# First batch of a long convolution: loads further ahead, products made earlier and shared by two engines, half of a sign change on another engine

## The chip, the cores and the metric

One Trainium2 chip, one of its cores. TensorE (PE) multiplies matrices into PSUM; VectorE (DVE), ScalarE (ACT) and GpSimd (POOL) work element by element; SyncE (SP) and GpSimd issue the DMAs here. Each engine takes its instructions in the order in which the program lists them, and waits on semaphores of the others. The metric is the device time of one execution in microseconds; less is better.

## The reference

A long convolution over the sequence, multiplied by x, and a feed-forward net with a squared ReLU behind it:

```python
h_filt = (np.maximum(pos_emb @ w1, 0.0) @ w2) * np.exp(-0.01 * pos)[:, None]
u = x * v                                    # batch 4, seq 12480, d_model 128
Uf = np.fft.rfft(u, n=2 * S, axis=1)
Hf = np.fft.rfft(h_filt, n=2 * S, axis=0)
y = np.fft.irfft(Uf * Hf[None], n=2 * S, axis=1)[:, :S]
x = (x * y).reshape(B * S, D)
out = np.maximum(x @ w_in, 0.0) ** 2 @ w_out # 128 -> 2048 -> 128
```

All of it is in fp32.

## The kernel before

The sequence is padded to 112 x 112, and the transform is made of matmuls with tables of 112 x 112, in stages over one large SBUF tile `W`. Each fp32 operand is split into a high and a low part, and a product is three matmuls (`mm3`, lines 75 to 77). The order at the start of the program is: the filter's small net (`filter_mlp`), the filter's stage one (`stage1(None, True, ...)`, called `s1f`), the filter's stage two (`stage2(True, True, ...)`, `s2f`), the first batch's stage one (`stage1(0, True, ...)`, `s1`), its stage two, stage three, and then the feed-forward net, between whose steps the other batches' stages run. Only the filter's and the first batch's stages have nothing else beside them ("big").

Stage one goes over 32 blocks of 4 channels, 112 x 4 x 112 floats each. For a block of the first batch: `load` fetches xt and vt (lines 236, 237, SP's queue), `mul` makes u = x v in place of xt (244), `prep` makes the high part on ACT (254), `prep2` the low part on VectorE (262), `mm` issues 12 matmuls into two PSUM banks, and `evac` copies both banks into `W`, the first on ACT (282), the second on VectorE (280) where the stage is "big". The filter's stage one has no loads and no products. Stage two goes over 56 blocks. In the filter's, a block is: a half-precision table (load 344) widened on VectorE (`widen`, 363), a block of `W` split into high part (`prep`, ACT, 385) and low part (`prep2`, VectorE, 393), its real part's sign changed (`neg`: line 401 on GpSimd for the filter, 403 on ACT otherwise), 12 matmuls, and a copy by ACT (423) that is stored to `Hd` (424). `prep` and `prep2` run two blocks ahead of the matmuls.

No planner sets the order: the stages are Python generators, and whoever advances one with `step` places its next section in every engine's queue at that point. A `hook` is called at the end of each block with t - n, so t == -28 is block 4 of 32 in stage one and t == -3 is block 53 of 56 in stage two. Before the first block, stage one has sections that end in a `yield`: the first loads; then the first products and the remaining early loads; then the first `prep`; then the first `prep2`. In the kernel before, the filter's stage one places the first section of `s1`, and block 53 of the filter's stage two the second one, with three products.

Of the kernel before, what the change touches and what calls it, by code (L numbers as in the profile page):

```python
# [7 lines left out]
F32 = mybir.dt.float32  # L8
# [9 lines left out]
I = 112  # L18
# [14 lines left out]
def hyena_moe_kernel(  # L33
# [19 lines left out]
    nc = tc.nc  # L53
# [12 lines left out]
    def pool(name, side="left", **kw):  # L66
        return tc.tile_pool(name=name, bufs=kw.pop("bufs", 2), side=side, reuse_waits="tile", **kw)

    def bank():
        return psf.tile([128, 512], F32, tag="F", name="F")  # L70

    def mm3(o, L, R, first=True, last=True):
        lh, ll = L
        rh, rl = R
        nc.tensor.matmul(o, lh, rh, start=first, stop=False)  # L75
        nc.tensor.matmul(o, lh, rl, start=False, stop=False)  # L76
        nc.tensor.matmul(o, ll, rh, start=False, stop=last)  # L77

    def load_tab(p, src, k):
        t = p.tile([I, k, 2 * I], F32R, name="tab", bufs=1)  # L80
        nc.gpsimd.dma_start(out=t, in_=src)
        return t
# [50 lines left out]
    def by_value():  # L133
        return W.rearrange("p t (c d) -> p (t c) d", c=4)
# [4 lines left out]
    def first_rows():  # L139
        return W.rearrange("p t (q d) -> p (t q) d", q=4)[:, :I].rearrange("p (e s) (c k) -> p c e s k", e=4, k=4)  # L140
# [73 lines left out]
    def rest(k):  # L214
        for _ in range(k):
            yield 1
            yield 2
            yield 3

    def stage1(b, big, et=None, side="left", hook=None):  # L220
        DC = 4
        n = D // DC
        with pool("s1", side) as p:
            if et is None:
                et = load_tab(p, e_tab, 2)
            E = (et[:, 0, :], et[:, 1, :])
            ext = 3 if big else 0
            pa = (3 if b is None else 2) if big else 1
            L = {}

            def load(t):
                if b is None or t >= n:
                    return
                xt = p.tile([I, DC, I], F32, tag="xt", name="xt", bufs=2 + pa + ext)
                vt = p.tile([I, DC, I], F32, tag="vt", name="vt", bufs=2 + ext)
                nc.sync.dma_start(out=xt, in_=xs[b, :, t * DC : (t + 1) * DC, :])
                nc.sync.dma_start(out=vt, in_=vs[b, :, t * DC : (t + 1) * DC, :])
                L[t] = xt, vt

            def mul(t):  # L240
                if b is None or t >= n:
                    return
                xt, vt = L[t]
                nc.gpsimd.tensor_mul(out=xt, in0=xt, in1=vt)

            def like(x):
                return x if b is not None else x.rearrange("p d (s k) -> p d s k", k=4)

            def prep(t):
                if t >= n:  # L250
                    return
                u = first_rows()[:, t] if b is None else L.pop(t)[0]
                hi = p.tile([I, DC, I], F32R, tag="uh", name="uh", bufs=1 + pa)
                nc.scalar.copy(like(hi), u)
                q[t] = u, hi

            def prep2(t):
                if t >= n:
                    return
                u, hi = q[t]  # L260
                lo = p.tile([I, DC, I], F32R, tag="ul", name="ul", bufs=1 + pa)
                nc.vector.tensor_sub(out=like(lo), in0=u, in1=like(hi).bitcast(F32))
                q[t] = hi, lo

            def mm(t):
                hi, lo = q.pop(t)
                A = []
                for h in range(DC // 2):
                    A.append(bank())
                    for k in range(2):  # L270
                        mm3(A[h][:I, k * 2 * I : (k + 1) * 2 * I], (hi[:, 2 * h + k, :], lo[:, 2 * h + k, :]), E)
                return A

            def evac(t, A):
                for h in range(DC // 2):
                    d0 = t * DC + 2 * h
                    dst = by_value()[:, :, d0 : d0 + 2]
                    src = A[h][:I, : 4 * I].rearrange("p (d t) -> p t d", d=2)
                    if big and h:
                        nc.vector.tensor_copy(dst, src)  # L280
                    else:
                        nc.scalar.copy(dst, src)

            q = {}
            la = 2 + pa + ext
            early = min(la, 2 + ext)
            for t in range(early):
                load(t)
            if big:
                yield 1  # L290
            else:
                yield from rest(1)
            for t in range(pa + 1):
                mul(t)
            for t in range(early, la):
                load(t)
            yield 1
            for t in range(pa):
                prep(t)
            yield 2  # L300
            for t in range(pa):
                prep2(t)
            prev = None
            for t in range(n):
                yield 1
                load(t + la)
                mul(t + pa + 1)
                if prev is not None:
                    evac(t - 1, prev)
                prep(t + pa)  # L310
                yield 2
                prep2(t + pa)
                yield 3
                prev = mm(t)
                if hook is not None:
                    hook(t - n)
            yield 1
            evac(n - 1, prev)

    def stage2(filt, big, side="left", ring=None, hook=None):  # L320
        n = I // 2
        TK = 2 if big and not filt else 1
        pa = 2 if big else 1
        lag = 2 if big else 1
        la = (4 if filt else 2 * (NTB - 1)) if big else 2
# [3 lines left out]
        def whole(t):  # L329
            return big and not filt and (t // TK % 2 == 1 or t >= n - 4)  # L330
# [24 lines left out]
        with pool("s2", side) as p:  # L355
# [39 lines left out]
            def neg(t):  # L395
                if t >= n or whole(t):
                    return
                a = q[t].rearrange("p h k r d -> p (h k) r d")
                src = a[:, :, 0, :].bitcast(F32)
                if filt:  # L400
                    nc.gpsimd.tensor_scalar(out=a[:, :, 2, :], in0=src, scalar1=-1.0, scalar2=1.0, op0=ALU.mult, op1=ALU.mult)
                else:
                    nc.scalar.mul(a[:, :, 2, :], src, -1.0)
# [49 lines left out]
            for t in range(pa):  # L453
                neg(t)
            prev = {}
            for t in range(n + lag):
                yield 1
                load(t + la)
                load_h(t + lh)
                prep(t + pa)  # L460
                yield 2
                if not big:
                    prep2(t + pa)
                if t - lag in prev:
                    post(t - lag, prev.pop(t - lag))
                if big:
                    prep2(t + pa)
                    widen(t + pa)
                yield 3
                neg(t + pa)  # L470
                if t < n:
                    prev[t] = mm(t)
                if hook is not None:
                    hook(t - n)
# [59 lines left out]
    def stage4(b, done, ring=None):  # L534
        L, X, q, Y, Z = {}, {}, {}, {}, {}

# [93 lines left out]
    def fft(b, done):  # L630
        yield from stage1(b, False)
        yield from stage2(False, False)
        yield from stage3(False)
        yield from stage4(b, done)
# [19 lines left out]
    def step(gen, k=1):  # L654
        for _ in range(k):
            next(gen, None)
# [4 lines left out]

    filter_mlp(tables)
    et = tabs[0]
    s1f = stage1(None, True, et, "right", lambda t: t == -28 and step(s1))
    s2f = stage2(True, True, "right", half, lambda t: t == -3 and step(s1))
    s1 = stage1(0, True, et, "left", lambda t: t == -3 and step(s2))
    step(s2f)
    run(s1f)
# [238 lines left out]
```

## Time and profile before

| | us |
|---|---|
| median of 3 runs | 3440.4 (3438.72 to 3444.68) |
| profiled execution | 3440.29 |
| its span, first to last instruction | 3438.5 |

Over the span TensorE is busy 99%, VectorE 82%, ScalarE 79%, GpSimd 40%; the mean granted clock is 0.993. The first 340 us hold the filter and the first batch; what follows is mostly the feed-forward net. Times in rows are microseconds, the start of an instruction counted from the span's start; an instruction's time holds what it waits for inside the engine, and in square brackets stands the idle time before it with what ended it.

### The profile page before, as it was taken

To read this page: it belongs to the slowest core of one execution; us is meant where nothing else is said; L and a number is where in the kernel's file an instruction comes from. 1 tells how busy PE (TensorE), PEld (TensorE's weight loads), DVE (VectorE), ACT (ScalarE), POOL (GpSimd) and SP (SyncE) were. 2 spreads that over 40 slices of the span, in tenths; PEclk is the share of its full clock that TensorE was granted. 3 is DMA by queue.
4 is the path that set the end of the run, shared out by engine and by line. 5 is a ranking of instruction groups with operands and counts; after the bars stand their busy time and mean duration, and the time that the engine had idled before them with its cause. 6 is when DMAs were issued, how large, how long until landed. Compare 5 with 4: busy or idle time off the path is not lost.

```text
span 3438.5 us, 58656 instructions
## 1 busy us (share of the span) xinstructions
PE 3390.6 (99%) x20986; PEld 3197.9 (93%) x20986; DVE 2830.0 (82%) x3328; ACT 2717.6 (79%) x4014; POOL 1370.2 (40%) x1448
## 2 busy tenths in 40 slices
PE   8998999999999999999999999999999999999999
PEld 8987999999999989999999999999999999999998
DVE  7989877889887777879887777788887777788888
ACT  6765778887778878887777788888777788888887
POOL 2578055349920045339940035436960015400000
PEclk9999999999999999999999999999999999999999
DMA  2899155446610055436630035445640025400000
GB/s 77 260 252 248 51 142 146 124 124 178 181 54 17 17 137 146 121 116 179 183 86 17 17 100 145 126 125 151 183 137 17 17 60 146 125 27 25 25 25 20
DMA packets 211892, 371.90 MB, mean 108 GB/s; under 512 B 26448, under 2 KB 156816, under 8 KB 211600
## 3 DMA queue, kind: packets, MB, share of 16 engines
q1 hardware_dynamic: 158736, 242.89, 24.1%
q0 software_dynamic: 52864, 125.27, 14.0%
q8 instruction: 166, 2.72, 0.3%
q14 instruction: 126, 1.03, 0.1%
HBM read 242.64 MB, written 64.00 MB: 89 GB/s over the span
## 4 chain that ended last, share of the span: by engine, by line
PE 86%; issue 8%; DVE 3%; DMA 1%; POOL 1%; ACT 1%; SPq 0%; DVEq 0%; POOLq 0%; ACTq 0%
PE F L75 11%; PE F L76 11%; PE F L77 11%; PE A L75 10%; PE A L77 10%; PE A L76 9%; PE O L75 8%; PE O L76 8%; PE O L77 8%; PE F L594 1%; DVE m L433 1%; DMA ht<-Hd 1%; PE F L593 1%; DVE W L433 1%; DMA vt<-vs 0%
## 5 line engine op out<-in xcount | busy, mean ns | idle before, releaser
L722 ACT ACTIVATE r<-A 128x892 f32<-128x892 f32 x896 | 821.8, 917 | 304.9 <-PE A L77 93.1
L725 DVE SCALAR_TENSOR_TENSOR A<-A,r 128x892 f32<-128x892 f32 x723 | 791.4, 1095 | 297.5 <-ACT r L722 295.3
L724 ACT ACTIVATE gh<-r 128x892 fp32r<-128x892 f32 x896 | 852.0, 951 | 186.2 <-PE O L77 179.6
L735 DVE TENSOR_TENSOR gl<-A,gh 128x892 fp32r<-128x892 f32 x723 | 786.0, 1087 | 143.2 <-ACT gh L724 120.2
L75 PE MATMUL A<-zh,wt 128*128 128x446 f32 x1792 | 675.6, 377 | 3.7 <-DVE gl L735 1.8
L77 PE MATMUL A<-zh,wt 128*128 128x446 f32 x1792 | 653.6, 365 | 0.0
L76 PE MATMUL A<-zl,wt 128*128 128x446 f32 x1792 | 651.7, 364 | 0.0
L541 POOL DMA_DIRECT2D tb<-t x224 | 123.9, 554 | 1083.4 <-PE F L77 828.6
L75 PE MATMUL O<-gh,wt 128*128 128x446 f32 x1456 | 529.5, 364 | 0.0
L77 PE MATMUL O<-gh,wt 128*128 128x446 f32 x1456 | 529.5, 364 | 0.0
L76 PE MATMUL O<-gl,wt 128*128 128x446 f32 x1456 | 529.3, 364 | 0.0
L75 PEld LDWEIGHTS A<-zh,wt 128*128 128x128 f32 x1792 | 344.3, 192 | 25.6 <-DVE gl L735 8.2
L77 PEld LDWEIGHTS A<-zh,wt 128*128 128x128 f32 x1792 | 336.8, 188 | 23.3
L76 PEld LDWEIGHTS A<-zl,wt 128*128 128x128 f32 x1792 | 340.1, 190 | 15.0 <-DVE zl L707 0.4
L567 POOL TENSOR_TENSOR al<-W,ah 112x512 fp32r<-112x512 f32 x212 | 288.0, 1358 | 70.6 <-ACT ah L565 56.4
L75 PE MATMUL F<-a,tb 112*112 112x256 f32 x1000 | 289.0, 289 | 11.7 <-DVE m L433 4.3
L76 PEld LDWEIGHTS O<-gl,wt 128*128 128x128 f32 x1456 | 275.6, 189 | 19.1
L75 PEld LDWEIGHTS O<-gh,wt 128*128 128x128 f32 x1456 | 274.7, 189 | 18.8
L77 PEld LDWEIGHTS O<-gh,wt 128*128 128x128 f32 x1456 | 273.0, 187 | 18.7
L76 PE MATMUL F<-a,tb 112*112 112x256 f32 x1000 | 282.6, 283 | 0.4 <-DVE a L393 0.4
L77 PE MATMUL F<-a,tb 112*112 112x256 f32 x1000 | 281.2, 281 | 0.0
L75 PE MATMUL F<-tab,vh 112*112 112x224 f32 x1024 | 276.4, 270 | 3.7 <-ACT vh L489 3.7
(113 smaller groups left out, 7685.7 us busy)
## 6 DMA issues: line engine op xcount, KB each, us to landing
tb<-t POOLq DMA_DIRECT2D x168, 392.0 KB, 3.5
ht<-Hd SPq DMA_DIRECT2D x224, 224.0 KB, 2.9
tb<-t POOLq DMA_DIRECT2D x224, 196.0 KB, 2.6
xt<-xs SPq DMA_DIRECT2D x128, 196.0 KB, 2.8
vt<-vs SPq DMA_DIRECT2D x128, 196.0 KB, 3.0
xt<-x SPq DMA_DIRECT2D x224, 112.0 KB, 2.2
zd<-zs SPq DMA_DIRECT2D x112, 223.0 KB, 2.4
out<-ot SPq DMA_DIRECT2D x112, 223.0 KB, 2.3
```

The lines of the kernel that those rows point to most:

```text
L75: nc.tensor.matmul(o, lh, rh, start=first, stop=False)
L76: nc.tensor.matmul(o, lh, rl, start=False, stop=False)
L77: nc.tensor.matmul(o, ll, rh, start=False, stop=last)
L433: nc.vector.tensor_mul(out=m[r], in0=Uv, in1=ht[:, :, :, r : r + 1].to_broadcast([I, D, 2, 2]))
L541: nc.gpsimd.dma_start(out=tb, in_=t1[:, t, :, :])
L567: eng.tensor_sub(out=lo, in0=w, in1=hi.bitcast(F32))
L593: nc.tensor.transpose(A[:, I - 1 : PT], z[:, :, 1], ident)
L594: nc.tensor.transpose(A[:, :I], z[:, :, 0], ident)
L722: nc.scalar.activation(r, h, AF.Relu)
L724: nc.scalar.activation(hi, r, AF.Square)
L725: nc.vector.scalar_tensor_tensor(out=g, in0=h, scalar=0.0, in1=r, op0=ALU.max, op1=ALU.mult)
L735: nc.vector.tensor_sub(out=lo, in0=g, in1=hi.bitcast(F32))
```

## The change

`stage1` of the first batch (`first`) gets ten xt buffers instead of seven (five vt as before), so ten blocks are loaded ahead; five products instead of three are made before its first block (`ma`); of the others GpSimd makes those whose number divides by three and VectorE the rest; inside a block the product now stands ahead of the load; of the second PSUM banks VectorE copies those of odd blocks, and ACT those of even blocks. The sections of `s1` are placed one step earlier: the first loads at block 2 and the five products with loads 5 to 9 at block 10 of the filter's stage one, so that block 53 of the filter's stage two now places the first two `prep`. In the filter's stage two GpSimd keeps the sign change of odd blocks, and ACT makes that of even blocks.

```diff
-            ext = 3 if big else 0
+            first = big and b is not None
+            ext = 6 if first else 0
             pa = (3 if b is None else 2) if big else 1
+            ma = 5 if first else pa + 1
...
-                vt = p.tile([I, DC, I], F32, tag="vt", name="vt", bufs=2 + ext)
+                vt = p.tile([I, DC, I], F32, tag="vt", name="vt", bufs=5 if first else 2)
...
-                nc.gpsimd.tensor_mul(out=xt, in0=xt, in1=vt)
+                eng = nc.vector if first and t >= ma and t % 3 else nc.gpsimd
+                eng.tensor_mul(out=xt, in0=xt, in1=vt)
...
-                    if big and h:
+                    if big and h and (b is None or t % 2):
                         nc.vector.tensor_copy(dst, src)
...
-            early = min(la, 2 + ext)
+            early = min(la, 5 if first else 2)
...
-            for t in range(pa + 1):
+            for t in range(ma):
                 mul(t)
...
                 yield 1
+                mul(t + ma)
                 load(t + la)
-                mul(t + pa + 1)
...
-                if filt:
+                if filt and t % 2:
                     nc.gpsimd.tensor_scalar(out=a[:, :, 2, :], in0=src, scalar1=-1.0, scalar2=1.0, op0=ALU.mult, op1=ALU.mult)
                 else:
                     nc.scalar.mul(a[:, :, 2, :], src, -1.0)
...
-    s1f = stage1(None, True, et, "right", lambda t: t == -28 and step(s1))
+    s1f = stage1(None, True, et, "right", lambda t: t in (-30, -22) and step(s1))
```

## Rows read from the trace of the kernel before

**Rows 1.** The page's head.

```profile
span 3438.5 us, 58656 instructions
```

**Rows 2.** Windows by stage: stretch, its length, each engine's busy time, clock, DMA.

```profile
43.00:86.00 43.00, 41.71 (x384) 41.33 (x384) 37.05 (x64) 34.28 (x64) 0.00 (x0) 0.96 0.00 1
86.00:175.00 89.00, 87.10 (x672) 83.88 (x672) 86.64 (x112) 61.53 (x112) 53.65 (x58) 0.98 0.81 253
175.00:229.00 54.00, 48.67 (x384) 44.47 (x384) 49.71 (x64) 36.41 (x65) 44.16 (x34) 0.91 0.91 257
229.00:338.00 109.00, 97.26 (x552) 78.99 (x552) 104.60 (x155) 57.86 (x112) 93.73 (x106) 0.98 1.06 258
```

**Rows 3.** Timeline, filter's stage two, by engine: start, time, line, tiles.

```profile
160.50 1.09 DVE L393 TENSOR_TENSOR a<-W,a 112x512 fp32r<-112x512 f32 x1
161.52 0.61 DVE L363 CAST tb<-half 112x896 fp32r<-112x896 f16 x1
162.06 1.09 DVE L393 TENSOR_TENSOR a<-W,a 112x512 fp32r<-112x512 f32 x1
...
161.68 0.93 POOL L401 TENSOR_SCALAR a<-a 112x512 fp32r<-112x512 f32 x1 [0.62 <-DVE a L393]
...
160.98 0.62 ACT L385 CAST a<-W 112x512 fp32r<-112x512 f32 x1 [0.44 <-PE F L77]
161.50 0.58 ACT L423 COPY he<-F 112x512 f32<-112x512 f32 x1
```

**Rows 4.** Groups of instructions by line, 100 to 172 us: count, busy, mean.

```profile
L393 DVE TENSOR_TENSOR a<-W,a 112x512 fp32r<-112x512 f32 x47 | 51.4, 1094 | 0.0
```

**Rows 5.** Timeline, start of the first batch's stage two, VectorE and ACT.

```profile
234.37 0.69 DVE L393 TENSOR_TENSOR a<-W,a 112x512 fp32r<-112x512 f32 x1 [0.37 <-ACT a L385]
...
235.09 0.63 ACT L403 ACTIVATE a<-a 112x512 fp32r<-112x512 f32 x1 [0.76 <-DVE a L393]
235.63 0.60 ACT L385 CAST a<-W 112x512 fp32r<-112x512 f32 x1
```

**Rows 6.** Timeline, start of the batch's stage one, and one later place.

```profile
177.35 4.41 POOL L244 TENSOR_TENSOR xt<-xt,vt 112x448 f32<-112x448 f32 x4
...
177.18 5.07 DVE L262 TENSOR_TENSOR ul<-xt,uh 112x448 fp32r<-112x448 f32 x1
...
182.30 0.53 PE L77 MATMUL F<-tab,ul 112*112 112x224 f32 x1 [3.01 <-DVE ul L262]
...
236.34 3.37 DVE L393 TENSOR_TENSOR a<-W,a 112x512 fp32r<-112x512 f32 x1
```

**Rows 7.** Timeline, middle of the batch's stage one, VectorE and GpSimd.

```profile
201.48 0.61 DVE L280 COPY W<-F 112x448 f32<-112x448 f32 x1
202.02 1.04 DVE L262 TENSOR_TENSOR ul<-xt,uh 112x448 fp32r<-112x448 f32 x1
...
201.04 1.53 POOL L244 TENSOR_TENSOR xt<-xt,vt 112x448 f32<-112x448 f32 x1
```

**Rows 8.** Timeline, ACT, two instructions close together in the batch's stage one.

```profile
189.41 0.58 ACT L282 COPY W<-F 112x448 f32<-112x448 f32 x1
189.96 0.57 ACT L254 CAST uh<-xt 112x448 fp32r<-112x448 f32 x1
```

**Rows 9.** Timeline, end of the filter's net, by engine; landing of the vt loads.

```profile
34.62 1.98 POOL L160 TENSOR_TENSOR sl<-pt,sh 128x448 fp32r<-128x448 f32 x1 [0.41 <-ACT sh L159]
...
36.99 0.62 DVE L160 TENSOR_TENSOR sl<-a,sh 128x448 fp32r<-128x448 f32 x1
...
39.39 0.62 DVE L160 TENSOR_TENSOR sl<-a,sh 128x448 fp32r<-128x448 f32 x1
...
42.44 1.97 ACT L254 CAST uh<-W 112x448 fp32r<-112x448 f32 x4 [3.93 <-DVE W L186]
...
33.40 0.31 SPq L237 DMA_DIRECT2D vt<-vs  x1
...
DMA to landing us min/median/max: 4.6/5.4/5.6
```

## The prediction

> **What bounds the kernel now.** The page's head gives the span that the sum is made against, 3438.5 us [rows 1]; the profiled execution took 3440.29 us in all, 1.8 us more, and 0.1 us less than the median of the runs, 3440.4. Over the span TensorE is never idle for long, so a share of the whole says nothing: I read the busy time by stage next [rows 2]. The change touches three of those stretches. In the filter's stage one (43 to 86 us) TensorE is busy 41.71 of 43.00 us and GpSimd does nothing. In the filter's stage two (86 to 175 us) VectorE is busy 86.64 of 89.00 us. In the first batch's stage one (175 to 229 us) TensorE is busy only 48.67 of 54.00 us, although its 384 matmuls are as many and as wide as those of the filter's stage one, and its granted clock is 0.91: about 9.7 us at the lower of its two levels, 1.2 instead of 2.4 GHz, which alone costs some 4.9 us.
>
> The timeline of the filter's stage two tells what VectorE is full of [rows 3]. L393 (the low part, two SBUF inputs) takes 1.09 us, where the same instruction takes 0.69 us when GpSimd is quiet [rows 5]; the grouped row shows that all 47 of a long stretch do (mean 1094 ns), with no idle time before them [rows 4]. GpSimd's negation L401 runs from 161.68 to 162.61, and the L393 issued at 162.06 ends at 163.15, 0.54 us after it: it stood still until the negation was through. So a block costs VectorE 162.06 - 160.50 = 1.56 us.
>
> The start of the batch's stage one has the same thing at its worst [rows 6]: four products in a row on GpSimd (177.35 to 181.76) keep one L262 on VectorE for 5.07 us, TensorE waits 3.01 us for it, and the clock falls in the low stretch told above. Later the two alternate [rows 7]: a product takes 1.53 us instead of the 1.10 us of those four (4.41/4), L262 1.04 instead of 0.62. One block is then one product, 1.53 us.
>
> **The change, part by part.**
>
> *Five products before the filter's stage one.* GpSimd has nothing queued between its last L160 (ends at 36.60) and the filter's stage two, so mul(0) to mul(4) start there, whatever the hook's block says; their blocks are loaded (the last vt issued at 33.40, landing 4.6 to 5.6 us later) [rows 9]. Five by 1.10 us reach to 42.1. VectorE has two L160 with two SBUF inputs in that time, at 36.99 and 39.39, and the filter MLP's end hangs on them: the second one, then L186, then ACT's first L254 at 42.44 [rows 9]. Lower bound: each waits for the product that is under way, the first until 37.70, 0.7 us, most of which the L186 behind it spends waiting anyway, the second at most 1.0: together 0.6 to 1.6. Upper bound: the first is shut out by all five, as L262 was by four and an L393 for 3.37 us at 236.34 [rows 6]: 42.1 - 37.0 = 5.1 us, and with TensorE idle that long again some 6 us at the lower clock, 3 us more: 8. Between the ends I take **+3 us**. The SBUF page of the Trainium skill (SBUF — State Buffer, section "Who interferes with whom") says that such a VectorE instruction and a GpSimd instruction that reads SBUF exclude each other, and that the later one waits out the other's whole instruction. The trace agrees that it blocks, but 5.07 us is four instructions, not one; by the rule alone this term would be 1.6 and the sum 1.4 us lower.
>
> The five pairs of loads for blocks 5 to 9 go out on SP at the same time (before, blocks 5 and 6 went out in the third-last block of the filter's stage two, the rest in the batch's own). Each vt load waits on SP for a product, and behind it stand the fifth half table and then the filter's Hd stores, none needed before 86 us: nothing.
>
> *Every second negation on ACT.* This puts an instruction that waits for VectorE into ACT's queue, ahead of ACT's next L385, and the next L393 waits for that. The first batch's stage two has the same order today [rows 5]: L393 ends at 235.06, the negation starts on ACT at 235.09, the next L385 at 235.63. From the end of an even block's L393 to that of the odd block's: 0.03 + 0.54 + 0.62 for L385 [rows 3] + 0.03 + 0.69 for an L393 that nothing holds up = 1.91 us, where 1.56 were. The odd block's negation is still on GpSimd, and the L393 after it belongs to an even block, whose L385 has no negation ahead of it: it starts 0.52 + 0.58 after the odd one's L385 [rows 3], so is done in time, and today's order (L393, L363, the negation, L393) comes back: 1.56. A pair of blocks takes 3.47 instead of 3.12. Over 26 pairs: **+9 us**. Lower bound: the even L393 gets ahead of GpSimd's negation; then the second half is two VectorE slots, 0.54 + 0.54, the pair takes 2.99, and the term is -3.4. Upper bound: two blocks of the start and end also lose, +10.
>
> *The batch's stage one.* No products stand at its start, and ten blocks are loaded, so TensorE begins as stage two's last matmul ends: the stall and the low clock go. The two L254 now sit in ACT's queue in stage two's last blocks, 1.14 us by 0.57 [rows 8]; ACT is busy 61.53 of 89.00 us there [rows 2], so that costs nothing; without that cover 1. From then on the pace is set by the slowest of three:
> - ACT: per two blocks two L254 and three copies (the even blocks' second copy is now its own). One follows the other after 0.55 us [rows 8], at most 0.57: 1.38 to 1.43 us a block.
> - VectorE: per six blocks six L262, four products and three copies, 13 slots of 0.54 (202.02 - 201.48 [rows 7]): 7.0 us. Two products on GpSimd hold it up by what L262 waits now, 1.04 - 0.62 = 0.42 us, to 0.96 where no copy fills the time: 7.9 to 8.9, or 1.31 to 1.49 us a block.
> - TensorE: 41.71/32 = 1.30 [rows 2].
>
> ACT and VectorE are both nearly full and in one chain, so I take 1.45 rather than the larger mean: 32 x 1.45 + 0.6 for the last copy = 47.0 against 54.0: **-7 us**. Bounds: 1.30 gives 42.2 and -11.8; today's 1.53 gives 49.6 and -4.4.
>
> The loads are then needed at 1.45 us a block instead of 1.53, for 22 blocks instead of 25 or 27. Traffic in that stretch is 257 GB/s and the next stretch moves 258 [rows 2]; two loads of 112 x 4 x 112 floats in 1.45 us are 277 GB/s. A lag of 0.1 us a block would add up to 2 us in 22 blocks, less than the five blocks by which they are ahead: hidden.
>
> *Sum*: 3440.3 + 3 + 9 - 7 = 3445.3; **3445 us**.
>
> **The rivals.**
> - *The negation pays (faster).* If the even block's L393 reaches the port before GpSimd's negation, the term is -3.4: 3440.3 + 3 - 3.4 - 7 = 3433. It decides at one place, the order of these two after each odd block's L363. For it: that L393 stands ready 0.47 us after the odd one's end (162.06 - 161.59 [rows 3]). Against: the negation starts 0.09 us after it (161.68), and won in every one of 47 [rows 4].
> - *The five products shut VectorE out.* The first term is 8: 3450. For it: both long rows [rows 6]. Against: in the steady stretch L262 gets its turn after each product [rows 7].
> - *The port stays the bound.* VectorE and GpSimd only swap products that need the same port; stage one's pace stays at 1.53, only the stall goes: -4.4, and 3448. For it: today's alternation [rows 7]; against: two thirds of GpSimd's 1 us turns become 0.54 us ones. The Trainium skill warns of it (Perfetto Trace Analysis, section "Optimizing Scalar/DVE Operations": moving work between these two might not help, since they share a read port); the trace bears it out for L262.
>
> **How the numbers follow.** The forecast's case has 0.47 and, with its terms a little off, lies between 3439 and 3450. The negation that pays has 0.17, the shut-out 0.21, the port as bound 0.15. The range takes in the first rival and the second with a few us: 3431 to 3454. A difference of 0.2% (6.9 us, 3433.5 to 3447.3) is about what a measurement of this kernel tells from no change. Faster than that is most of the first rival, 0.14; slower is the forecast's upper end and most of the shut-out and of the port's case, 0.34; within it 0.52.
>
> **What would show it.** In the trace after: L393 by turns at about 0.69 and 1.09 us and the filter's stage two some 98 us long instead of 89; if it is 85 or less, the second term was wrong. Products at 36.6 us on GpSimd, with an L160 of 1.2 us or more beside them; an L160 of 4 us or more is the shut-out. In the batch's stage one no gap before the first matmul, a granted clock of 1.00, ACT nearly full, 46 to 48 us; at 42 TensorE sets the pace and the third term was too small. A stage two of the first batch that is longer than its 109 us by more than 2 us would be a cost that I have not counted.

## The result and the profile after

The changed kernel takes 3460.7 us (median of four runs, 3459.42 to 3464.22), against 3439.9 for the kernel before, timed beside it: a ratio of 1.0063, 95% interval 1.005 to 1.0075. It is slower by some 21 us, on the side that had 0.34, and above the range. The span says the same:

```profile
span 3458.2 us, 58562 instructions
```

The windows by stage, on the same stretches as [rows 2], then finer in the batch's stage one (stretch, its length, busy time of PE, PEld, DVE, ACT and POOL, granted clock, DMA share, GB/s):

```profile
43.00:86.00 43.00, 40.18 (x384) 39.81 (x384) 37.56 (x66) 35.46 (x66) 1.05 (x1) 1.00 0.11 33
86.00:175.00 89.00, 78.98 (x610) 73.99 (x611) 72.17 (x105) 66.76 (x127) 24.08 (x26) 0.98 0.77 234
175.00:229.00 54.00, 41.83 (x327) 39.71 (x326) 37.95 (x57) 35.58 (x69) 11.39 (x11) 0.86 0.63 190
...
184.00:196.00 12.00, 11.35 (x104) 10.78 (x104) 11.36 (x19) 11.17 (x23) 1.87 (x2) 1.00 0.84 255
196.00:206.00 10.00, 5.56 (x53) 5.29 (x51) 4.80 (x10) 6.35 (x13) 1.30 (x1) 0.86 0.60 179
...
218.00:230.00 12.00, 7.92 (x40) 7.65 (x41) 7.66 (x12) 4.71 (x9) 2.47 (x2) 0.60 0.54 168
```

The filter's stage two got through 610 of its 672 matmuls in the 89 us in which it had made all of them. The batch's stage one begins well: 104 matmuls in 12 us are 1.38 us a block, the three engines of the chain are all above 90%, and the clock is whole. Then every engine has much idle time, TensorE, VectorE, ScalarE and the DMA engines alike (179 and 168 GB/s against 255), and the granted clock falls to 0.60: the stage waits for something that no engine is busy with.

By the first and last matmul of each of the first three stages in the timelines; the batch's stage two is counted to the first matmul of stage three, and stage three to the first matmul of the feed-forward net:

| us | before | after |
|---|---|---|
| filter's stage one | 43.05 to 84.96 | 43.90 to 84.32 |
| filter's stage two | 87.73 to 174.83 (87.1) | 87.10 to 183.79 (96.7) |
| batch's stage one, from the end of the stage ahead of it | to 228.55 (53.7) | to 250.95 (67.2) |
| batch's stage two | to 339.69 (111.1) | to 362.16 (111.2) |
| stage three | to 434.09 (94.4) | to 455.91 (93.7) |

So +9.6 in one stage and +13.5 in the next, and some 3 us less elsewhere. The chain of the first, in the timeline of the filter's stage two (it answers to [rows 3]):

```profile
94.91 1.10 DVE L396 TENSOR_TENSOR a<-W,a 112x512 fp32r<-112x512 f32 x1
...
97.22 0.69 DVE L396 TENSOR_TENSOR a<-W,a 112x512 fp32r<-112x512 f32 x1 [0.67 <-ACT a L388]
...
98.36 1.10 DVE L396 TENSOR_TENSOR a<-W,a 112x512 fp32r<-112x512 f32 x1
...
96.05 0.64 ACT L406 ACTIVATE a<-a 112x512 fp32r<-112x512 f32 x1 [0.82 <-DVE a L396]
96.59 0.60 ACT L388 CAST a<-W 112x512 fp32r<-112x512 f32 x1
```

L396 ends at 96.01, ScalarE's sign change (L406) has waited 0.82 us for it and starts, the next high part (L388) stands behind it, and VectorE idles 0.67 us until that is done. A pair of blocks takes 98.36 - 94.91 = 3.45 us.

For the second, who waited for whom in 184 to 251 us (in total, times, longest), and the same of SyncE's queue:

```profile
POOL xt L247 <- DMA vt<-vs: 31.7, 5, 8.3
ACT W L285 <- PE F L77: 22.9, 17, 5.5
DVE xt L247 <- DMA vt<-vs: 20.3, 11, 4.0
...
SPq L239 <- DMA vt<-vs: 22.8, 7, 3.6
SPq L239 <- POOL xt L247: 10.0, 7, 1.7
```

The products wait for vt to land, but SyncE, which issues the loads, waits too: seven vt loads (L239) first for the landing of another vt and then for GpSimd's product of it, 32.8 us in all. The timeline shows one such round and the start of the next:

```profile
187.70 0.38 SPq L239 DMA_DIRECT2D vt<-vs  x1
...
189.11 0.39 SPq L238 DMA_DIRECT2D xt<-xs  x1
194.20 0.31 SPq L239 DMA_DIRECT2D vt<-vs  x1
...
195.03 0.42 SPq L239 DMA_DIRECT2D vt<-vs  x1
195.54 0.38 SPq L238 DMA_DIRECT2D xt<-xs  x1
200.25 0.31 SPq L239 DMA_DIRECT2D vt<-vs  x1
...
193.03 1.14 POOL L247 TENSOR_TENSOR xt<-xt,vt 112x448 f32<-112x448 f32 x1 [8.30 <-DMA vt<-vs]
198.93 1.30 POOL L247 TENSOR_TENSOR xt<-xt,vt 112x448 f32<-112x448 f32 x1 [4.75 <-DMA vt<-vs]
...
203.08 0.63 DVE L247 TENSOR_TENSOR xt<-xt,vt 112x448 f32<-112x448 f32 x1 [3.87 <-DMA vt<-vs]
```

The vt of block 12 goes out at 187.70. GpSimd's product of it ends at 193.03 + 1.14 = 194.17, and 0.03 us later SyncE, which had stood still since 189.50, issues the vt of block 14. The vt of block 15 goes out at 195.03; its product ends at 200.23, and block 16's vt leaves at 200.25. From there one vt load in three is held like that, up to 237.81: five rounds of three blocks in 37.6 us, 2.5 us a block where the engines could do 1.4. The buffers say why. These are the SBUF addresses that the program as built gives to the vt tiles, of the kernel after and of the first experiment below:

```
block:       10     11     12     13     14     15     16     17     18     19
after:   154496 161664 156288 159872 156288 158080 158080 154496 161664 161664
own:     161664 159872 154496 158080 163456 156288 161664 159872 154496 158080
```

In the kernel after the five buffers are not used in turn (in the kernels before, all_dve and all_pool, where one engine makes the products from block 5 on, they are; what decides the order is not shown). Block 14 gets block 12's, 16 gets 15's and 19 gets 18's: the buffer of a block that GpSimd multiplies goes straight to the next or next but one load. That load must wait until the block ahead has landed and been multiplied, and all loads behind it on SyncE wait as well. However far ahead a load is listed, the loads now come in rounds of three.

### The profile page after: what moved, and what is told of

It reads as the page before. It is cut to its first block, busy times and chain, and to the rows that moved or that the text cites. A ratio compares the mean times of both kernels' runs of the same rounds, so it can differ in the third digit from the quotient of the medians.

```text
span 3458.2 us, 58562 instructions
## 1 busy us (share of the span) xinstructions
PE 3390.6 (98%) x20986; PEld 3198.1 (92%) x20986; DVE 2808.8 (81%) x3330; ACT 2737.0 (79%) x4058; POOL 1317.7 (38%) x1402
## 4 chain that ended last, share of the span: by engine, by line
PE 83%; issue 9%; DVE 4%; DMA 2%; ACT 1%; POOL 1%; SPq 0%; DVEq 0%; POOLq 0%; ACTq 0%
PE F L75 10%; PE F L76 10%; PE F L77 10%; PE A L75 10%; PE A L77 10%; PE A L76 9%; PE O L75 8%; PE O L76 8%; PE O L77 8%; DVE a L396 1%; DMA ht<-Hd 1%; DMA vt<-vs 1%; PE F L597 1%; DVE m L436 1%; PE F L596 1%
```

## The experiments

The theory (buffer) is what the last paragraph says. The rivals for the lost 13 us were that VectorE and GpSimd hold each other up (port), ScalarE with its extra copies, and the order or depth of the loads as such. All experiments were timed in five rounds beside the kernel before, which had 3440.8 us in the first four and 3439.6 in the last four. Stage lengths are from one profile each, measured as in the table above:

| | time, us | ratio to before (95%) | filter's stage two | batch's stage one |
|---|---|---|---|---|
| before | 3439.9 | | 87.1 | 53.7 |
| after | 3460.7 | 1.0063 (1.005 to 1.0075) | 96.7 | 67.2 |
| own | 3438.4 | 0.9995 (0.9986 to 1.0004) | 96.7 | 45.6 |
| six | 3446.7 | 1.0021 (1.0012 to 1.003) | 96.9 | 56.6 |
| all_dve | 3445.7 | 1.0014 (1.0005 to 1.0023) | 96.7 | 52.8 |
| neg_only | 3448.5 | 1.0023 (1.0013 to 1.0033) | 96.6 | 53.6 |
| own_neg_back | 3429.7 | 0.9972 (0.9962 to 0.9982) | 87.0 | 45.8 |
| own_late | 3425.3 | 0.9963 (0.995 to 0.9975) | 82.7 | 46.1 |
| all_dve_hold | 3441.0 | 1.0005 (0.9996 to 1.0014) | 96.6 | 48.5 |
| all_pool | 3442.8 | 1.0011 (1.0002 to 1.002) | 96.6 | 50.6 |

**Separate buffers for each engine's blocks (own).**

```diff
-                vt = p.tile([I, DC, I], F32, tag="vt", name="vt", bufs=5 if first else 2)
+                vt = p.tile([I, DC, I], F32, tag="vg" if first and t % 3 == 0 else "vt", name="vt", bufs=(2 if t % 3 == 0 else 4) if first else 2)
```

> The kernel after, with the vt buffers split by the engine that makes the product: two for blocks whose number divides by three (GpSimd), four for the others (VectorE), so that each group is used in turn. Theory (buffer): in the kernel after, a vt load is put into the buffer that the latest GpSimd block has just been loaded into, so SyncE waits for that landing and that product, and every load behind it waits too; with separate groups the loads flow, the batch's stage one takes 46 to 48 us instead of 67, and the time is about 3440 us (3437 to 3444). Rival (port): the two engines that share the products hold each other up, and the buffers only show it; stage one stays above 60 us and the time above 3455. Rival (ScalarE): the second copies of even blocks make ScalarE the bound; stage one also stays above 60 us.

The stage takes 45.6 us, a little less than the 46 to 48 of the theory, and the kernel 3438.4, within it; both rivals fall, since the split of products and ScalarE's copies are those of the kernel after. Its windows, and SyncE's waits for its vt loads in 184 to 251 us:

```profile
184.00:230.00 46.00, 42.04 (x382) 40.18 (x380) 41.37 (x65) 40.46 (x79) 11.92 (x10) 1.00 0.94 270
...
SPq L239 <- DMA vt<-vs: 2.6, 9, 0.5
```

22.8 us of waiting for a landing have become 2.6 (none of them longer than 0.5), and the wait for GpSimd's product, 10.0 us, is gone. The clock is 1.00 through the stage.

**One buffer more, in one group (six).** Own has six buffers, one more than the kernel after, so this is its control.

```diff
-                vt = p.tile([I, DC, I], F32, tag="vt", name="vt", bufs=5 if first else 2)
+                vt = p.tile([I, DC, I], F32, tag="vt", name="vt", bufs=6 if first else 2)
```

> The kernel after with six vt buffers in one group instead of five, the control for the run with separate groups, which has six as well. Theory (buffer): the order of reuse is what counts; with six in one group the buffer just filled for GpSimd's block is still the one taken next (vt of block 17 goes where block 15's went), so stage one stays above 58 us and the time above 3451 us. Rival (number): five were simply too few for ten blocks ahead; then six bring stage one down by several us, as in the run with separate groups, to about 3440.

56.6 us and 3446.7: between the two, and below what I had set for the theory (58 us, 3451). The number of buffers does matter: it brings 10.6 of the 21.6 us that own brings. The order brings the other 11. The same waits are there, shorter, because the load that is held now has one or two others between itself and the one that it waits for (block 15 goes where 12 was, 17 where 15 was):

```profile
SPq L239 <- DMA vt<-vs: 12.0, 6, 2.8
SPq L239 <- POOL xt L247: 7.8, 6, 1.4
```

**All products from block 5 on VectorE (all_dve).** One engine frees the five buffers in turn.

```diff
-                eng = nc.vector if first and t >= ma and t % 3 else nc.gpsimd
+                eng = nc.vector if first and t >= ma else nc.gpsimd
```

> The kernel after with all products from block 5 on VectorE, none on GpSimd; five vt buffers in one group, which one engine then frees in turn. Theory (buffer): loads flow; VectorE has per two blocks two L265, two products and one copy, five slots of 0.54, 1.35 us a block, ScalarE 1.40, so stage one takes 45 to 47 us and the time is 3438 to 3442 us. Rival (port): the same result, since GpSimd is quiet. Rival (ScalarE): stage one stays above 60 us and the time above 3455. Rival (load rate): ten blocks ahead or the product ahead of the load is what starves the loads, whoever multiplies; above 60 us too.

This missed: 52.8 us, not 45 to 47. The loads were late here too, but for another reason. The timeline of VectorE and GpSimd, and the list of DMA issues in 190 to 204 us (KB each, median us from issue to landing):

```profile
203.62 0.63 DVE L247 TENSOR_TENSOR xt<-xt,vt 112x448 f32<-112x448 f32 x1 [3.86 <-DMA vt<-vs]
...
189.94 1.12 POOL L350 DMA_DIRECT2D tb<-t  x2 [6.58 <-ACT uh L257]
...
tb<-t POOLq DMA_DIRECT2D x2, 784.0 KB, 10.5
vt<-vs SPq DMA_DIRECT2D x6, 196.0 KB, 11.0
xt<-xs SPq DMA_DIRECT2D x5, 196.0 KB, 12.6
```

and of own, the timeline of GpSimd and the same list:

```profile
218.09 1.10 POOL L350 DMA_DIRECT2D tb<-t  x2
...
vt<-vs SPq DMA_DIRECT2D x11, 196.0 KB, 5.2
xt<-xs SPq DMA_DIRECT2D x10, 196.0 KB, 5.2
```

GpSimd's queue holds the table loads of the batch's stage two behind its products. Without products it issues them 28 us earlier, twice 784 KB amid the x and v loads, and those land after 11 to 12.6 us instead of 5.2. VectorE, which now has a product at the head of its queue, stands still for 3.86 us.

**The tables held back (all_dve_hold).** GpSimd makes one product, that of block 30, ahead of its table loads.

```diff
-                eng = nc.vector if first and t >= ma else nc.gpsimd
+                eng = nc.vector if first and t >= ma and t != 30 else nc.gpsimd
```

> The kernel with all products from block 5 on VectorE, save that of block 30, which GpSimd makes, ahead of its table loads for the batch's stage two. Theory (tables): without products GpSimd issued two table loads of 784 KB at 189.9 us instead of 218.1, in the middle of the x and v loads, which then took 9 us instead of 5 to land, and VectorE's queue stood still behind a product for 3.9 us. With one product ahead of them the tables go out at about 217 us, the stage takes 45 to 48 us instead of 52.8, and the time is 3438 to 3441 us. Rival (VectorE full): with all products VectorE cannot keep the pace, the stage stays at 51 us or more and the time at 3444 or above.

```profile
219.43 1.14 POOL L247 TENSOR_TENSOR xt<-xt,vt 112x448 f32<-112x448 f32 x1 [36.42 <-DMA vt<-vs]
220.53 1.09 POOL L350 DMA_DIRECT2D tb<-t  x2
...
220.60 0.31 SPq L239 DMA_DIRECT2D vt<-vs  x1
...
vt<-vs SPq DMA_DIRECT2D x11, 196.0 KB, 5.4
xt<-xs SPq DMA_DIRECT2D x10, 196.0 KB, 5.6
```

By its timelines and its DMA issues in 190 to 204 us, the tables leave at 220.53 and the landing time is back at 5.4 us. The stage takes 48.5 us, 0.5 more than the tables' theory allowed, and the kernel 3441.0, at its upper edge. VectorE was not too full; most of the miss was the tables. What is left shows the buffers once more: the vt of block 31, the last one, leaves at 220.60, 0.03 us after GpSimd's product of block 30 ends (219.43 + 1.14), because it is given that block's buffer.

**All products on GpSimd (all_pool).**

```diff
-                eng = nc.vector if first and t >= ma and t % 3 else nc.gpsimd
+                eng = nc.gpsimd
```

> The kernel after with all products on GpSimd, as in the kernel before, five vt buffers in one group, the rest of the change kept. Theory (buffer): one engine frees the buffers in turn and the loads flow; the pace is GpSimd's product by turns with VectorE's L265, 1.53 us a block as in the kernel before, so the batch's stage one takes 46 to 50 us and the time is 3440.8 + 9.6 - 4 to 8 = 3443 to 3447 us. Rival (load rate or order): ten blocks ahead, or the product ahead of the load in a block, starves the loads whoever multiplies; stage one above 58 us and the time above 3452.

50.6 us and 3442.8 us, each just outside the first theory (46 to 50, 3443 to 3447) and far from the rival's 58 and 3452. Ten blocks ahead and a product ahead of the load starve nothing; it takes two engines freeing one group of buffers. What the 5 us more than own's 45.6 are, the windows tell, of all_pool, own and the kernel before, and the timeline of the start of the stage in all_pool:

```profile
184.00:195.00 11.00, 7.70 (x52) 7.51 (x51) 7.64 (x6) 5.50 (x11) 7.41 (x8) 0.69 0.88 271
195.00:225.00 30.00, 28.01 (x250) 26.30 (x249) 28.85 (x31) 27.31 (x52) 25.93 (x20) 1.00 0.89 256
...
184.00:195.00 11.00, 10.35 (x95) 9.78 (x94) 10.41 (x18) 10.39 (x21) 2.23 (x2) 1.00 1.01 318
195.00:225.00 30.00, 27.35 (x251) 26.26 (x250) 28.36 (x45) 26.39 (x53) 9.69 (x8) 1.00 1.04 287
...
195.00:225.00 30.00, 29.98 (x246) 26.57 (x245) 30.00 (x43) 23.11 (x42) 29.52 (x21) 1.00 0.90 251
...
182.96 5.52 POOL L247 TENSOR_TENSOR xt<-xt,vt 112x448 f32<-112x448 f32 x5
...
182.78 7.26 DVE L265 TENSOR_TENSOR ul<-xt,uh 112x448 fp32r<-112x448 f32 x3
...
189.03 0.53 PE L77 MATMUL F<-tab,ul 112*112 112x224 f32 x1 [3.30 <-DVE ul L265]
```

In 195 to 225 us the three make 250, 251 and 246 matmuls, 12 to a block: 1.44, 1.43 and 1.46 us a block. The pace is the same, whoever multiplies. The 5 us are lost at the start, where all_pool makes 52 matmuls and own 95 in 11 us, at 1.4 us a block some 5 us of work. Blocks 5 to 9 lie loaded, GpSimd multiplies them in one row of 5.52 us, three L265 beside it take 7.26 us, TensorE waits 3.30 us for one of them, and the granted clock is 0.69: the stall of [rows 6] again.

**The sign change alone (neg_only).** The kernel before with the one line:

```diff
-                if filt:
+                if filt and t % 2:
```

> The kernel before with one part of the change: in the filter's stage two ScalarE makes the sign change of even blocks. Theory (the second step of the prediction): a pair of blocks takes 3.47 us instead of 3.12, the filter's stage two 96.5 us instead of 87, and the time is 9 to 10 us above the kernel before, 3449 to 3450 us. Rival: the 9.6 us seen in the kernel after come from its other parts (loads or products placed elsewhere), and this kernel stays within 3 us of the kernel before.

Its filter's stage two takes 96.6 us, and its batch's stage one, where nothing was changed, 53.6. The time is 8 us above before, a little under the 9 to 10 expected; the mechanism needs nothing of the rest of the change.

**Separate buffers without the sign change (own_neg_back).** Own, with that line as it was before.

> The kernel with separate vt buffers, and every sign change of the filter's stage two on GpSimd again. Theory: the two mechanisms are separate and add up. The filter's stage two takes 87 us instead of 96.7, the batch's stage one 45 to 47, and the time is 3438.4 - 9.6 = 3429 us (3426 to 3433), below both the kernel before and the kernel after. Rival: what one stage gains the next gives back (at 1.40 us a block the loads have no slack, and a filter's stage two that is 10 us shorter leaves them less time), and the time stays above 3434.

3429.7 us, as expected, with stages of 87.0 and 45.8: the two mechanisms add up, and the loads keep their pace when the stage ahead of them is 10 us shorter. This is faster than both kernels, 0.28% below the kernel before.

**ScalarE's sign change one block later (own_late).** Own, and in the filter's stage two:

```diff
                 prep(t + pa)
+                if filt and (t + pa) % 2 and t + pa > pa:
+                    neg(t + pa - 1)
...
-                neg(t + pa)
+                if not filt or t % 2:
+                    neg(t + pa)
```

> The kernel with separate vt buffers, and ScalarE's sign change of an even block placed one block later in its queue, behind the next block's high part (L388). Theory: the sign change on ScalarE costs because it waits for the low part at the head of ScalarE's queue, ahead of the next high part; placed behind that, it costs only its own 0.54 us. ScalarE then has 2.9 us per pair of blocks and VectorE about 2.8 to 3.0 (one L396 of the pair is free of GpSimd), so the filter's stage two takes 80 to 86 us instead of 96.7 and the time is 3422 to 3429 us. Rival: VectorE and GpSimd still exclude each other for both low parts, or ScalarE's 0.54 us count in full; the stage stays at 90 us or more and the time above 3431.

3425.3 us, the fastest: 0.37% below the kernel before, 35 us below the kernel after. The timeline of the filter's stage two, its L396 grouped (100 to 160 us), and its window:

```profile
150.69 0.63 ACT L388 CAST a<-W 112x512 fp32r<-112x512 f32 x1
151.38 0.63 ACT L406 ACTIVATE a<-a 112x512 fp32r<-112x512 f32 x1
151.91 0.57 ACT L426 COPY he<-F 112x512 f32<-112x512 f32 x1
...
L396 DVE TENSOR_TENSOR a<-W,a 112x512 fp32r<-112x512 f32 x41 | 34.2, 834 | 0.3
...
86.00:170.00 84.00, 81.91 (x676) 80.92 (x677) 77.16 (x114) 73.87 (x141) 27.12 (x31) 0.98 0.86 269
```

The next high part now stands ahead of the sign change, and VectorE's idle time in front of L396 is 0.3 us over 41 blocks. L396 takes 0.83 us in the mean instead of the 1.09 of [rows 4], for every second one is free of GpSimd (by turns 1.00 and 0.68 us in the timeline at 150 us). So the idea behind the sign change was sound and its place was not: the same instruction on the same engine costs 9.6 us in one place and brings 4.4 in the other (82.7 against 87.1).

## Why the prediction was wrong

**Five products before the filter's stage one: +3 taken, nothing measured.** The products ran where the prediction put them, and the L160 beside them took these times in the timeline of the kernel after:

```profile
37.20 6.86 POOL L247 TENSOR_TENSOR xt<-xt,vt 112x448 f32<-112x448 f32 x5
...
37.63 0.62 DVE L160 TENSOR_TENSOR sl<-a,sh 128x448 fp32r<-128x448 f32 x1
...
40.01 0.84 DVE L160 TENSOR_TENSOR sl<-a,sh 128x448 fp32r<-128x448 f32 x1
```

One of the two was 0.22 us longer than in [rows 9]; the shut-out did not happen, and GpSimd paid instead: five products took 6.86 us, not 5 x 1.10 = 5.5. The Trainium skill (SBUF — State Buffer, section "SBUF: two separate sides") has the later of the two wait out the other's whole instruction; here the first L160, issued while the products ran, took its usual 0.62 us and the second 0.84, while the 5.07 us of [rows 6] remain more than it allows. With all products on GpSimd it went the other way: the five took 5.52 us and three L265 beside them 7.26. What decides which of the two gives way is not shown. The first matmul's shift (43.05 to 43.90) isn't the products' either: neg_only, which has none there, starts at 43.87, and six, which has them, at 42.88.

**Every second negation on ACT: +9 taken, 9.6 measured.** The pair took 3.45 us where 3.47 was worked out, by the order that the prediction told: the negation waits for VectorE at the head of ScalarE's queue. Neg_only shows it alone. The rival that the negation pays did not occur.

**The batch's stage one: -7 taken, +13.5 measured. Here it failed.** Not in the pace: as long as loads lasted it was 1.38 us a block, and with the buffers in turn the whole stage took 45.6 us against the 47.0 that I had, -8.1. (The pace came out near the 1.45 that I took; but the kernel before had it too, and nearly all of the -8.1 is the stall at the start, as the paragraph on the port tells.) What failed is the last step, that the loads are ahead and their lag "hidden". I compared the rate of the traffic with that of the need and took the depth of ten blocks as given. I did not ask which buffer each vt load would be put into, and on whose product it would wait. The diff had both halves of the answer: ten xt buffers but still five vt, and two engines that free them. No view of the trace before could show it, since there one engine made all products; the place to look was the wait that each vt load would carry and where its product stands. Own and six tell the price: 21.6 us of the stage, of which one more buffer removes half.

**The port as bound.** The pace stayed, as this rival said, but it was never 1.53: that is the time of one product in [rows 7], where the kernel before makes a block in 1.46 us. With the buffers in turn, two thirds of the products on VectorE brought 0.03 us a block, 1 us in the stage. That leaves some 7 us for the start, where the row of products is gone; the rival had 4.4 for it. That all_pool's 50.6 us lie near the rival's 49.6 is chance: its pace is 1.44, and a row of five at the start costs the rest.

**No gap before the first matmul, the clock at 1.00.** The gap was gone and the clock whole until 196 us, as foretold; behind the waits for loads it fell to 0.60 in 218 to 230 us. The rest of the first batch was unchanged, 111.2 us for stage two.

**The sum.** With the terms as measured, 3440.3 + 0 + 9.6 + 13.5 = 3463.4, where the profiled execution took 3460.3: the 3 us are the filter's stage one (-0.6), stage three (-0.7) and what follows it (-1.8). With the buffers in turn it is 3440.3 + 9.6 - 8.1 = 3441.8; own's profiled execution took 3442.7, its median 3438.4. What follows the first batch, where no kernel differs, varies between these profiles by some 4 us, without an order that I could explain; that stays open, and differences of a few us between single profiles are not read here.

## What to carry to other kernels

Prefetch depth is what the buffers' reuse lets through, not how many loads stand early in the program: with two engines freeing one group of buffers, look up which buffer each load gets and what it must wait for, and give each engine's blocks a group of their own. An instruction that waits at the head of an in-order queue costs what stands behind it, so moving it one place back can be worth more than moving it to another engine. Emptying a queue also sets free the transfers that it was holding back. And a stage's pace is read apart from its start: here sharing the products left the pace as it was, and what it gained was a start without a row of them.

## What the runs showed that I had not expected

- Where ScalarE's instruction stands in its queue was worth 14.0 us over 56 blocks (96.7 against 82.7), more than which engine does it (87.0 with all on GpSimd).
- Two table loads of 784 KB, issued 28 us earlier because GpSimd had nothing ahead of them, doubled the landing time of 196 KB loads from 5.2 to 11 us and more.
- The filter's stage one came in two forms, whatever the kernel. In the kernel before, six, all_dve, all_dve_hold and all_pool the first matmul stands at 42.9 to 43.3 us, a low stretch of the clock follows at 44 to 45 us for 3.4 us, and the stage ends at 84.8 to 85.2; in the others it starts at 43.8 to 43.9, without that low stretch, and ends at 84.2 to 84.3. A later start ended earlier by some 0.6 us. What decides between the two was not tried.
